# New planned durations and a newly searched order for a linear-attention and token-mixing kernel

## The chip, the cores and the metric

The kernel runs on one core of one Trainium2 chip. The metric is the device time of one execution in microseconds; the kernel before has a median of 141.56 us over 3 runs. PE is the matmul engine (TensorE), DVE is VectorE, ACT is ScalarE, POOL is GpSimd, and SP is SyncE, which here only issues DMAs.

## The reference

Two stages follow each other. The first is a linear attention with a decaying state, over 4 batches, 8 heads, 768 positions and a head size of 48:

```python
for t in range(S):
    kt, vt, rt = (k[:, :, t], v[:, :, t], r[:, :, t])
    cur = np.einsum('bhd,bhe->bhde', u[None] * kt, vt)
    y[:, :, t] = np.einsum('bhd,bhde->bhe', rt, state + cur)
    state = w[None, :, :, None] * state + np.einsum('bhd,bhe->bhde', kt, vt)
```

The second takes its output as x (4 batches, 768 tokens, 384 channels) and mixes tokens with two 768x768 matrices and channels with two 384x384 ones:

```python
theta = x @ w_theta
zr, zi = x * np.cos(theta), x * np.sin(theta)
y = np.einsum('ts,bsd->btd', w_tok_r, zr) + np.einsum('ts,bsd->btd', w_tok_i, zi)
u = x + y
out = u + np.maximum(u @ w_ch, 0.0)
```

## The kernel before

The 768 positions of a batch are cut into 6 chunks of 128 rows, taken two at a time. There are 12 such pairs, counted 0 to 11, three to a batch. A pair's work is called its front. Its k, r and v are loaded from SP into a ring of 9 tiles `ld` (L492, L499). k and r are multiplied by powers of w into Kw and Rw (L663), transposed on PE against an identity matrix ("flip", L553), and evacuated from PSUM to KT and RT (L562 on DVE, L564 on ACT). KT times RT gives the scores (L702), which DVE multiplies with a mask into mAT (L708). PD is RT times KT elementwise (L715), and one small matmul group ("diag", L724) sums it to dg; dg times v is yd (L732). Kw times v, the outer products, gives the state's sums (L747, or L761 for pairs 0 to 3); the state goes to N (L801) and, in bf16, to Sb. For pairs 0 to 3 the rows of v arrive two to a partition; they are cast to v2 (L616, L618) and placed by "put" matmuls (L627). Sb and mAT give the outputs (L821, L830), which with yd become x (L838).

x is transposed to xT, either by a flip or, for pairs 6 to 10, by a DMA transpose from SP (L573). theta is three matmuls a chunk against Wth (L853), followed by cosine and sine on ACT (L858, L861), and DVE multiplies x with both into z (L864).

The mixing of a batch needs the z of all its pairs. For each of 6 output chunks it runs 3 groups of 4 matmuls ("mix", L884), one group for each pair's z. DVE adds x (u, L891, kept in the tile uu_all), u is transposed by DMA for pairs 0 to 10, three matmuls against Wch follow (L907, "chan"), DVE finishes (fin, L911, the tile fin_all) and SP stores (L917).

The four weight matrices are loaded and cast to bf16 by DMAs that POOL issues (L512): Wth and Wch in one piece each, each token matrix (Wr for w_tok_r, Wi for w_tok_i) in three pieces of two row blocks. A piece lands in a tile that is idle then (z, x, uu_all, fin_all), and PE flips each of its two blocks into WrT or WiT. All casts stand behind a small copy on POOL, the gate (L687), that waits until the load of pair 2's r has landed.

The order of all this is not that of the code. Every piece of work is a task of a plan (`P.add`), with an engine, a planned duration, what it reads and writes, and how many of the 8 PSUM banks it takes. `Plan.order()` runs a small event-driven plan of the five engines and the two DMA queues (SP's and POOL's): whenever an engine is free it takes, among the tasks whose inputs are ready, the one with the lowest number. The numbers come from the list `RANK`, one for each of the 698 tasks, and `MOVED` names the tasks that go to their alternative engine (DVE instead of POOL, ACT instead of DVE, and so on). The order in which the tasks come out is the order in which the instructions are put on each engine. So the planned durations have no effect on the chip other than through this order: each engine runs its own instructions strictly in it, and each instruction waits for its inputs as they really arrive. The assignment of PSUM banks follows from the same run.

In the plan of before a DMA's result is ready 2000 ns (`LANDING`) after its data have gone through the planned queue. When both queues have transfers, each goes on at the share that the transfer of POOL's queue gives: 0.2 for SP and 0.9 for POOL with Wth and Wch, 0.13 and 0.95 with the token matrices. Tasks that use the SBUF port that DVE and POOL share (`port=True`) exclude each other in the plan; on the chip such a POOL instruction also waits for the last such DVE instruction that precedes it in the order.

Of the kernel before, what the change touches and what calls it, by code (L numbers as in the profile page):

```python
# [23 lines left out]
LAT = {PE: 230.0, DVE: 150.0, ACT: 250.0, POOL: 170.0, SP: 0.0}  # L24
SWITCH = 95.0
LANDING = 2000.0


class Task:
# [5 lines left out]
class Plan:  # L35
# [50 lines left out]
    def order(self):  # L86
# [23 lines left out]
        while times or dma_next < math.inf:  # L110
# [7 lines left out]
            while dma_at < now:  # L118
                live = [q for q in (0, 1) if queues[q]]
                if not live:  # L120
                    dma_at = now
                    break
                rate = self.rates(queues)
                q = min(live, key=lambda q: todo[q] / rate[q])
                need = todo[q] / rate[q]
                step = need if dma_at + need <= now + 1e-6 else now - dma_at
                for i in live:
                    todo[i] -= step * rate[i]
                if dma_at + need <= now + 1e-6:
                    dma_at += need  # L130
                    t = queues[q].pop(0)
                    todo[q] = queues[q][0].xfer if queues[q] else 0.0
                    t.end = dma_at + LANDING
                    release(t.users, t.end)
                else:
                    dma_at = now
            for e in engines:
                if free_at[e] > now:
                    continue
                shut = e in port_free and port_free[POOL if e == DVE else DVE] > now  # L140
                nfree = sum(1 for b in banks if b[0] <= now)
                t = min((t for t in waiting[e] if t.ready <= now and not (t.port and shut)
                         and not (t.acq and len(t.acq) + t.spare > nfree)),
                        key=lambda t: (t.prio, t.seq), default=None)
                if t is None:
                    continue
                waiting[e].remove(t)
                banks.sort()
                for b in t.acq:
                    self.bank_of[b] = banks.pop(0)[1]  # L150
                ns = t.ns
                if e == PE:
                    ns += SWITCH if t.mode != last_mode else 0.0
                    last_mode = t.mode
                t.start, done = now, now + ns
                free_at[e] = done
                if t.port:
                    port_free[e] = done
                heapq.heappush(times, done)
                out.append(t)  # L160
                if t.xfer > 0:
                    q = int(e == POOL)
                    queues[q].append(t)
                    if len(queues[q]) == 1:
                        todo[q] = t.xfer + ns
                else:
                    t.end = done + LAT[e] - min(t.xfer, 0.0)
                    for b in t.uses:
                        left[b] -= 1
                        freed[b] = max(freed.get(b, 0.0), t.end)  # L170
                        if left[b] == 0:
                            banks.append((freed[b], self.bank_of[b]))
                            heapq.heappush(times, freed[b])
                    release(t.users, t.end)
                release(t.nexts, done)
# [12 lines left out]
CAST_AFTER = 7  # L188

RANK = [  # L190
# [38 lines left out]
]  # L229

MOVED = [
    30, 32, 74, 77, 92, 97, 99, 182, 213, 222, 242, 257, 275, 280, 287, 364, 365, 368, 377, 382,
    396, 399, 428, 440, 516, 520, 529, 548, 551, 560, 580, 592, 595, 689,
]


# [15 lines left out]
def kernel(  # L252
# [260 lines left out]
              wr=keys, prio=prio, xfer=xfer, share=share, name="cast")  # L513

    def square(src, dst, key, prio, after):
        cast(dst, src.rearrange("(o p) n -> p o n", p=C), [key], prio, 1870, (0.2, 0.9), after)

    z1 = zs[1].rearrange("p o t n -> p (o t n)")
    landing = [(z1[:, 4 * S:], [("z", 1, 2)]),
# [9 lines left out]
    def token_weights(after):  # L529
        for q in range(NP):  # L530
            for key, src, dst in (("Wr", moe_w_tok_r, WrT), ("Wi", moe_w_tok_i, WiT)):
# [5 lines left out]
                for to in (2 * q, 2 * q + 1):  # L537
                    if (key, to) in W_BY_DMA:
                        P.add(SP, 1250, lambda dst=dst, mid=mid, to=to:
                              nc.sync.dma_start_transpose(out=dst[:, :, to * C:(to + 1) * C],  # L540
                                                          in_=mid[:, to % 2, :]),
                              rd=keys, wr=[(key, to)], prio=60 + to, xfer=900, name="turn")
                        continue
                    flip(dst[:, :, to * C:(to + 1) * C],
                         [mid[:, to % 2, s * C:(s + 1) * C] for s in range(NCH)],
# [25 lines left out]
    def turn(dst, src, tok, prio, rd, wr, by_dma):  # L571
        if by_dma:
            P.add(SP, 1250, lambda: nc.sync.dma_start_transpose(  # L573
                out=dst, in_=src.rearrange("p t n -> p (t n)")), rd=rd, wr=wr, prio=prio,
                xfer=900, name="turn")
        else:
            flip(dst, [src[:, t, dk * C:(dk + 1) * C] for t in range(2) for dk in range(ND)],
                 tok, prio, rd, wr)
# [3 lines left out]
    def front(b, base):  # L582
# [59 lines left out]
        for pr in range(NP):  # L642
# [71 lines left out]
            def pairwise(eng, PD=PD, RT=RT, KT=KT):  # L714
                eng.tensor_mul(PD, RT, KT)  # L715
            P.add(DVE, dve_ns(2 * HP * C, 2.0), lambda f=pairwise: f(nc.vector), rd=kKT + kRT,
                  wr=[kP], prio=pb + 4, port=True, name="PD",
                  alt=(POOL, 190 + 1.65 * 2 * HP * C, True, lambda f=pairwise: f(nc.gpsimd)))
            td = ("dg", g)

            def diag(td=td, PD=PD):
# [256 lines left out]
```

## Time and profile before

| what | us |
|---|---|
| median of 3 runs | 141.56 |
| lowest and highest of them | 141.51, 141.77 |
| the profiled execution, on the device | 142.75 |
| its span, from the first to the last instruction | 141.0 |
| busy in that span: PE, DVE, ACT, POOL | 125.4, 107.3, 76.6, 63.7 |

The profile is of one execution, and its times count from the first instruction. A row of a timeline or of the chain of waits begins with its start and its length in us. A group's row gives, behind a first bar, its busy time in us and the mean of one instruction in ns, then the idle time before it. Matmuls are pipelined, so their rows overlap: the chain of waits shows them without the overlap. "To landing" is the time from the issue of a DMA to the moment its semaphore tells of the data.

### The profile page before, as it was taken

The numbers are of one execution on the slowest core, as the hardware profiler recorded it, in microseconds if no ns is written. First come the engines' busy times: TensorE is split into PE (matmuls) and PEld (weight loads), VectorE is DVE, ScalarE is ACT, GpSimd is POOL, SyncE is SP. The second block draws the span as 40 slices with busy tenths as digits, with TensorE's granted clock in tenths as the row PEclk, the third lists the DMA queues.
The fourth block names the chain that finished last, engine by engine and source line by source line (L and its number), as shares of the span: only waits on it lengthen the run. The fifth ranks groups of instructions, "written<-read, shape, count | busy, mean of one in ns | idle before, by whom it ended". The sixth has DMA issues, their size and how long they took to land.

```text
span 141.0 us, 4099 instructions
## 1 busy us (share of the span) xinstructions
PE 125.4 (89%) x1677; PEld 84.1 (60%) x1677; DVE 107.3 (76%) x203; ACT 76.6 (54%) x142; POOL 63.7 (45%) x55
## 2 busy tenths in 40 slices
PE   1599989587999999999999999949899999999980
PEld 1377856374677577765677566726566556665640
DVE  5396999696474699999999999857986196446490
ACT  7967989958947860799434628535263400340010
POOL 6025599968050298594683879972500000000000
PEclk9999999999999999999999999999999999999998
DMA  2899999999995999999997999979984305412644
GB/s 68 234 325 327 247 240 170 214 199 190 197 211 133 195 200 167 191 176 196 156 233 127 207 254 173 245 118 241 198 210 150 69 8 161 105 67 48 175 167 167
DMA packets 72637, 25.24 MB, mean 179 GB/s; under 512 B 67241, under 2 KB 72618, under 8 KB 72618
## 3 DMA queue, kind: packets, MB, share of 16 engines
q1 hardware_dynamic: 70186, 22.03, 78.0%
q0 software_dynamic: 2432, 2.95, 11.9%
q8 instruction: 13, 0.21, 0.7%
q14 instruction: 6, 0.05, 0.2%
HBM read 20.06 MB, written 4.72 MB: 176 GB/s over the span
## 4 chain that ended last, share of the span: by engine, by line
PE 51%; DMA 19%; DVE 15%; POOL 7%; issue 4%; ACT 2%; DVEq 0%; POOLq 0%
PE bank L884 24%; DMA x<-in_moe_w_tok_i_dram 9%; PE bank L553 6%; PE bank L853 6%; DVE mAT L708 6%; PE bank L907 6%; DMA uu_all<-uu_all 5%; DMA xT<-x 4%; POOL yd L732 2%; DVE Rw L663 2%; DVE fin_all L911 2%; PE bank L702 2%; POOL PD L715 1%; PE bank L830 1%; DVE x L838 1%
## 5 line engine op out<-in xcount | busy, mean ns | idle before, releaser
L884 PE MATMUL bank<-z,WrT 128*128 128x384 bf16 x144 | 46.9, 326 | 0.0
L884 PE MATMUL bank<-z,WiT 128*128 128x384 bf16 x144 | 46.8, 326 | 0.0
L708 DVE TENSOR_TENSOR mAT<-bank,mask 128x512 bf16<-128x512 f32 x48 | 31.1, 681 | 2.4 <-PE bank L702 2.4
L884 PEld LDWEIGHTS <-WrT 128*128 128x128 bf16 x144 | 14.0, 97 | 8.0
L864 DVE TENSOR_TENSOR z<-x,trig 128x1536 bf16<-128x1536 bf16 x12 | 12.4, 1036 | 8.3 <-ACT trig L858 4.9
L884 PEld LDWEIGHTS <-WiT 128*128 128x128 bf16 x144 | 14.1, 98 | 7.7
L861 ACT ACTIVATE trig<-bank 128x384 f16<-128x384 f32 x24 | 11.6, 492 | 11.3 <-PE bank L853 5.6
L564 ACT ACTIVATE KT<-bank 128x1024 bf16<-128x1024 bf16 (+1 forms) x12 | 11.9, 989 | 10.2 <-PE bank L553 6.5
L715 POOL TENSOR_TENSOR PD<-RT,KT 128x1024 bf16<-128x1024 bf16 x7 | 14.9, 2127 | 5.5 <-ACT RT L564 3.2
L732 POOL TENSOR_TENSOR yd<-dg,vb 128x768 bf16<-128x768 f32 x10 | 14.7, 1475 | 6.0 <-DVE Rw L663 2.5
L891 DVE TENSOR_TENSOR uu_all<-bank,x 128x384 bf16<-128x384 f32 x24 | 13.2, 552 | 4.7 <-PE bank L884 4.4
L663 POOL TENSOR_TENSOR Kw<-ld,kpow 128x768 bf16<-128x768 f32 x7 | 12.7, 1815 | 8.8 <-DVE z L864 7.2
L907 PE MATMUL bank<-Wch,uu_all 128*128 128x384 bf16 x72 | 14.7, 326 | 2.0 <-DMA uu_all<-uu_all 1.9
L853 PE MATMUL bank<-Wth,xT 128*128 128x384 bf16 x72 | 14.4, 327 | 2.2 <-DMA Wth<-in_moe_w_theta_dram 1.8
L911 DVE SCALAR_TENSOR_TENSOR fin_all<-bank,uu_all 128x384 f32<-128x384 f32 x24 | 12.9, 552 | 4.1 <-PE bank L907 2.2
L663 POOL TENSOR_TENSOR Rw<-ld,rpow 128x768 bf16<-128x768 f32 x6 | 10.9, 1815 | 10.0 <-DVE z L864 5.2
L858 ACT ACTIVATE trig<-bank,pi 128x384 f16<-128x384 f32 x24 | 13.3, 582 | 3.5 <-PE bank L853 3.4
L838 DVE TENSOR_TENSOR x<-bank,yd 128x384 bf16<-128x384 f32 x24 | 12.3, 548 | 1.3 <-PE bank L830 1.3
L564 ACT ACTIVATE RT<-bank 128x1024 bf16<-128x1024 bf16 (+1 forms) x11 | 10.8, 985 | 1.8 <-PE bank L553 1.7
L907 PEld LDWEIGHTS <-uu_all 128*128 128x128 bf16 x72 | 6.6, 98 | 6.7 <-DMA uu_all<-uu_all 2.5
L853 PEld LDWEIGHTS <-xT 128*128 128x128 bf16 x72 | 6.3, 98 | 6.4 <-DMA Wth<-in_moe_w_theta_dram 1.9
L553 PE MATMUL bank<-ident,Kw 128*128 128x128 bf16 x96 | 8.4, 235 | 1.9 <-DVE Kw L663 1.7
(104 smaller groups left out, 185.7 us busy)
## 6 DMA issues: line engine op xcount, KB each, us to landing
ld<-in_r_dram SPq DMA_DIRECT2D x12, 384.0 KB, 6.1
out_dram<-fin_all SPq DMA_DIRECT2D x11, 384.0 KB, 2.7
ld<-in_k_dram SPq DMA_DIRECT2D x16, 192.0 KB, 4.8
ld<-in_v_dram SPq DMA_DIRECT2D x16, 192.0 KB, 5.9
ld<-in_k_dram SPq DMA_DIRECT2D x4, 384.0 KB, 4.9
ld<-in_v_dram SPq DMA_DIRECT2D x4, 384.0 KB, 4.7
fin_all<-in_moe_w_tok_i_dram POOLq DMA_DIRECT2D x1, 384.0 KB, 8.2
z<-in_moe_w_tok_r_dram POOLq DMA_DIRECT2D x1, 384.0 KB, 9.9
```

Of the source, the lines that this page charges most:

```text
L553: nc.tensor.matmul(bank16(tok)[:, i * C:(i + 1) * C], s, ident, is_transpose=True, start=(i == 0), stop=(i == n - 1))
L564: nc.scalar.activation(dst, src, Act.Copy)
L663: eng.tensor_mul(X[:, :, hs, :D], src[:, :, hs], pw[:, :, hs])
L708: P.add(DVE, dve_ns(HP * C), lambda hi=hi, tk=tk, mAT=mAT: nc.vector.tensor_mul(mAT[:, hi], bank(tk[hi]).rearrange("p (h t) -> p h t", h=H ...
L715: eng.tensor_mul(PD, RT, KT)
L732: eng.tensor_mul(yd.rearrange("p a h d -> p (a h) d"), wide(dg, D), vb.rearrange("p a h d -> p (a h) d"))
L838: P.add(DVE, dve_ns(HD), lambda hi=hi, ty=ty, yd=yd, pr=pr: nc.vector.tensor_add(x[:, 2 * pr:2 * pr + 2].rearrange("p a (h i e) -> p a h i ...
L853: nc.tensor.matmul(bank(th)[:, :HD], xT[:, t, dk, :], Wth[:, dk, :], start=(dk == 0), stop=(dk == ND - 1))
L858: P.add(ACT, act_ns(HD, False) + 65 + (1300 if g == 0 and t == 0 else 0), lambda th=th, t=t, trig=trig: nc.scalar.activation(trig[:, t, 0] ...
L884: nc.tensor.matmul(bank(tm)[:, :HD], (WrT, WiT)[ri][:, so, to * C:(to + 1) * C], z[:, so, ri], start=(part == 0 and i == 0), stop=(part == ...
L907: nc.tensor.matmul(bank(tf)[:, :HD], uT[:, t, dk, :], Wch[:, dk, :], start=(dk == 0), stop=(dk == ND - 1))
L911: nc.vector.scalar_tensor_tensor(fin[:, t], bank(tf)[:, :HD], 0.0, un[:, t], op0=Alu.max, op1=Alu.add),
```

## The change

These planned quantities are changed:

- a matmul task that starts before 11.2 us of the plan is held for 1.8 times as long;
- the cast of Wth is held for 3370 ns of transfer instead of 1870, and while it runs SP's queue goes on at 0.4 and POOL's at 0.95 (before 0.2 and 0.9); Wch stays as it was;
- a DMA transpose's transfer is held for 1000 ns instead of 900;
- and its result comes 1300 ns later than before;
- the product PD on POOL costs 190 + 1.9 ns an element column instead of 190 + 1.65.

RANK and MOVED are replaced by new lists. The number of tasks and what each computes stay as they are. 36 of the 698 tasks are now on another engine.

```diff
 LANDING = 2000.0
+SLOW_UNTIL = 11200.0
+TURN_LATE = 1300.0
...
-                    t.end = dma_at + LANDING
+                    t.end = dma_at + LANDING + (t.share[1] if q == 0 else 0.0)
...
                 if e == PE:
                     ns += SWITCH if t.mode != last_mode else 0.0
+                    ns *= 1.8 if now < SLOW_UNTIL else 1.0
...
 RANK = [
-    0, 361, 360, 363, 362, 364, 365, 366, 369, 372, 377, 367, 370, 368, 371, 382, 397, 383, 384,
+    0, 413, 412, 415, 414, 416, 417, 418, 421, 424, 429, 419, 422, 420, 423, 434, 408, 435, 436,
...
 MOVED = [
-    30, 32, 74, 77, 92, 97, 99, 182, 213, 222, 242, 257, 275, 280, 287, 364, 365, 368, 377, 382,
-    396, 399, 428, 440, 516, 520, 529, 548, 551, 560, 580, 592, 595, 689,
+    32, 40, 74, 84, 89, 94, 99, 112, 163, 172, 193, 197, 210, 213, 222, 234, 242, 245, 247, 275,
+    278, 365, 396, 408, 428, 440, 516, 548, 551, 580, 602, 691,
 ]
...
-        cast(dst, src.rearrange("(o p) n -> p o n", p=C), [key], prio, 1870, (0.2, 0.9), after)
+        cast(dst, src.rearrange("(o p) n -> p o n", p=C), [key], prio, 1870 + 1500 * (key == "Wth"), (0.4, 0.95) if key == "Wth"
+             else (0.2, 0.9), after)
...
-                xfer=900, name="turn")
+                xfer=1000, share=(1.0, TURN_LATE),
+                              name="turn")
...
-                  alt=(POOL, 190 + 1.65 * 2 * HP * C, True, lambda f=pairwise: f(nc.gpsimd)))
+                  alt=(POOL, 190 + 1.9 * 2 * HP * C, True, lambda f=pairwise: f(nc.gpsimd)))
```

In the new order, among what the prediction speaks of: POOL has Rw of pair 1, yd of pair 0, the gate, the casts of Wth, Wr 2-3 and Wch, then Kw of pair 3, the casts of Wi 0-1 and Wr 0-1, N, and the cast of Wi 4-5; two PD, a yd and a v2 cast follow, and then the casts of Wr 4-5 and Wi 2-3. Before, it had a v2 cast, Rw of pairs 1 and 2, yd of pair 0 and N ahead of the gate, and then the casts of Wth, Wi 2-3, Wr 0-1, Wi 0-1, Wch and Wi 4-5. On PE the first mixing group is the 56th group of tasks where it was the 57th. On SP the loads keep their order among themselves; around them, the small second load of w, with that of u, moves behind the first load of r, and late in the kernel the load of r of pair 8 moves behind the DMA transposes of u of pair 3 and x of pair 7, and the transpose of u of pair 5 moves ahead of a store.

More of the change, by code (lines that the diff above doesn't have):

```diff
@@ L541, in token_weights @@
                                                           in_=mid[:, to % 2, :]),
-                              rd=keys, wr=[(key, to)], prio=60 + to, xfer=900, name="turn")
+                              rd=keys, wr=[(key, to)], prio=60 + to, xfer=1000, share=(1.0, TURN_LATE),
+                              name="turn")
                         continue
@@ L574, in turn @@
                 out=dst, in_=src.rearrange("p t n -> p (t n)")), rd=rd, wr=wr, prio=prio,
-                xfer=900, name="turn")
+                xfer=1000, share=(1.0, TURN_LATE),
+                              name="turn")
         else:
```

74 rows, old and new, of the table RANK are left out of this document.

## The prediction

> **What bounds the kernel now.** I read the engine shares first, then a table of busy time by stage, then what TensorE (PE) waits for.
>
> ```profile
> PE 125.4 (89%) x1677; PEld 84.1 (60%) x1677; DVE 107.3 (76%) x203; ACT 76.6 (54%) x142; POOL 63.7 (45%) x55
> ```
>
> ```profile
> core 0: us, PE busy (x) PEld busy (x) DVE busy (x) ACT busy (x) POOL busy (x), PEclk, DMA share, GB/s
> 0.00:15.35 15.35, 10.61 (x142) 7.68 (x143) 10.13 (x34) 12.06 (x26) 4.96 (x13) 1.00 0.90 244
> 15.35:36.50 21.15, 17.15 (x331) 12.60 (x332) 17.81 (x33) 18.25 (x35) 18.02 (x17) 1.00 1.12 204
> 36.50:92.50 56.00, 55.65 (x864) 38.61 (x863) 50.34 (x86) 33.65 (x59) 35.00 (x22) 1.00 1.11 189
> 92.50:104.00 11.50, 9.12 (x107) 5.57 (x105) 8.83 (x17) 5.71 (x12) 5.72 (x4) 1.00 1.17 197
> 104.00:135.00 31.00, 30.97 (x231) 18.76 (x229) 17.85 (x31) 6.42 (x15) 0.00 (x0) 1.00 0.38 103
> 135.00:141.00 6.00, 1.94 (x13) 0.84 (x11) 2.34 (x5) 0.49 (x1) 0.00 (x0) 0.90 0.53 197
> ```
>
> PE does the same matmuls in either order, so the end can move only by PE's idle time: the stage's length less its busy time. That is 4.7 us before 15.35, 4.0 from there to 36.5 (where the first mixing matmul starts), 0.4 from 36.5 to 92.5, 2.4 from 92.5 to 104, nothing to 135, 4.1 at the end. The head and the tail are mostly latency, so 6.4 us can be argued over.
>
> ```profile
> PE bank L907 <- DMA uu_all<-uu_all: 1.9, 1, 1.9
> PE bank L853 <- DMA Wth<-in_moe_w_theta_dram: 1.8, 1, 1.8
> ...
> PE bank L553 <- DMA x<-in_moe_w_tok_i_dram: 1.0, 1, 1.0
> ...
> PE bank L853 <- DMA xT<-x: 0.5, 1, 0.5
> ```
>
> Each row gives who waited for what, the total, the times and the longest. PE waited for casts of the weights (Wth, the tok_i block that lands in x) and for DMA transposes (uu_all, xT). The edits change the planned durations of just these transfers, and of the early matmuls. The edits of durations issue nothing themselves; what changes on the chip is the order of the tasks, and the engine of 36.
>
> **The head, 0 to 15.35.** Up to the outer products of pair 1 both orders give PE the same groups, except that put(1,0) is in there before and diag(0) after. Prices of PE groups without overlap come from the chain of waits:
>
> ```profile
> 13.85 0.45 PE bank L553 x8
> 14.29 0.33 PE bank L627 x2
> 14.62 0.73 PE bank L761 x32
> 15.34 0.30 PE bank L724 x8
> ...
> 43.05 0.34 PE bank L553 x6
> 43.39 0.49 PE bank L853 x3
> ...
> 48.08 0.33 PE bank L702 x8
> ...
> 53.46 0.30 PE bank L821 x16
> 53.76 0.51 PE bank L830 x16
> ```
>
> Put (0.33) against diag (0.30) is nothing. ACT now evacuates the first KT half ahead of two tables and takes the cast of v2(0) from POOL, so RT and v2 come later; PE has the two puts and the first outer products in front of the scores meanwhile. I take +0.2, with ends of -0.3 (one diag or put hidden) and +0.7 (twice a put of 0.33, shown).
>
> The plan now holds early matmuls for 1.8 times slower until 11.2 us.
>
> ```profile
> 7.70 1.07 PE L553 MATMUL bank<-ident,Rw 128*128 128x128 bf16 x8
> ...
> 13.68 0.61 PE L553 MATMUL bank<-ident,Rw 128*128 128x128 bf16 x8
> ```
>
> The same eight flips take 1.07 us at 7.70 and 0.61 at 13.68, so the factor is right for this execution. The Trainium skill (TensorE: Matmul & The Clock Gate, Part 1) speaks against planning by it: the slow start is ended by a free-running activity window, it says, its place differs from run to run, and one should not fit to a cold count. By that rule the head's term would scatter around +0.2; no single trace can show it.
>
> **The casts, 15.35 to 36.5.** The start of the casts is set by POOL's queue.
>
> ```profile
> 15.63 1.82 POOL L663 TENSOR_TENSOR Rw<-ld,rpow 128x768 bf16<-128x768 f32 x1 [3.06 <-PE bank L724]
> 17.41 1.48 POOL L732 TENSOR_TENSOR yd<-dg,vb 128x768 bf16<-128x768 f32 x1
> ...
> 19.29 0.18 POOL L687 COPY gate<-ld 1x1 f32<-1x1 f32 x1
> 19.41 0.94 POOL L512 DMA_DIRECT2D Wth<-in_moe_w_theta_dram  x1
> ...
> 23.27 0.74 POOL L512 DMA_DIRECT2D z<-in_moe_w_tok_i_dram  x1
> ```
>
> After the change Rw of pair 2 is on DVE and N stands behind six casts; only yd(0) is left ahead of the gate. Its dg comes from diag(0), which PE now does before the second scores: behind diag stand scores 0.3, the state's column sums (16 matmuls, 0.5 or so by the 0.73 of 32), two flips 0.9 and outer products 0.7 before 15.5, so diag ends near 13.1, yd runs from 13.3 to 14.8 and Wth's cast is issued at about 15.1 instead of 19.4. N, 4.3 us of casts later, feeds only outputs(2), 36 PE groups further on. Kw of pair 3 (now on POOL) stands between the third and the fourth cast; it is the next to be late if its load is.
>
> ```profile
> z<-in_moe_w_tok_i_dram POOLq DMA_DIRECT2D x1, 384.0 KB, 15.3
> ...
> Wth<-in_moe_w_theta_dram POOLq DMA_DIRECT2D x1, 288.0 KB, 6.8
> ```
>
> Wth landed 6.8 after its issue (26.2), the sixth cast 15.3 after its own (38.6): five casts in 12.4 us, 2.5 apart. From 15.1 on that gives Wth at 21.9, then Wr 2-3 at 24.4, Wch (smaller) at 26.5, Wi 0-1 at 29.0, Wr 0-1 at 31.5, Wi 4-5 at 34.0.
>
> PE's arrival in the new order: from 15.5, put x4 (1.3), flips x4 (1.8), outputs without a state half (0.7), outer (0.7), a TX flip (0.3), scores x2 (0.7), diag (0.3): 5.8, so the first theta is reached at 21.3 and waits 0.6. To the Wr 2-3 flips come theta x2, scores x2 and outputs: 2.4, at 24.3, no wait. To Wi 0-1 another 3.5 (three flip groups, scores x2, diag, put, theta, outer): 27.9, waits 1.1. To Wr 0-1 another 1.5: 30.5, waits 1.0. Then three flip groups and two outputs (2.6) end at 34.1, when Wi 4-5 is there. Idle 2.7 in place of 4.0, and mixing starts near 34.5. I take **-1.3**. Ends: -3.4 if only the first wait stands (idle 0.6), +2.0 in the rival below.
>
> **The transposes, 92.5 to 104.**
>
> ```profile
> 85.59 0.75 SPq L492 DMA_DIRECT2D ld<-in_r_dram  x1
> 86.44 1.00 SPq L917 DMA_DIRECT2D out_dram<-fin_all  x1
> 87.53 1.75 SPq L573 DMA_TRANSPOSE uu_all<-uu_all  x1
> ```
>
> ```profile
> 87.53 7.17 DMA uu_all<-uu_all
> ...
> 96.53 4.97 DMA xT<-x
> ```
>
> The transpose of u of pair 3 took 7.17 us to land, xT of pair 8 4.97; PE stood 1.9 and 0.5 for them. On SP the new order puts the 384 KB load of r (85.59 here) behind both transposes instead of ahead, and the transpose of u of pair 5 ahead of an output. Were u's transpose as fast as xT's 4.97 it would land at 92.5, just as PE gets there: 1.9 gone. If the delay is the other traffic as such, nothing goes. Idle goes to something between 0 and 2.4; I take the middle, **-1.2**.
>
> **Middle and tail.** From 36.5 to 92.5 PE idles 0.4, so there is nothing to gain. DVE takes 18 tasks of other engines and gives 16, of the same kinds (Rw, PD, yd, evacuations): no term. At the end, two channel matmul groups now stand behind the last mixing group, and the last flip's evacuation goes from ACT to DVE.
>
> ```profile
> 137.08 0.56 DVE L911 SCALAR_TENSOR_TENSOR fin_all<-bank,uu_all 128x384 f32<-128x384 f32 x1 [0.20 <-PE bank L907]
> ```
>
> Before: the last fin ends 137.64, 3.0 after the last mixing (134.65), with 2.1 us of PE work behind it: 0.9 over. After: PE has 3.3 behind it and DVE un, six fins and one flip's evacuation (0.35 or so), of 0.55 each, so 4.2: 0.9 to 1.0 over, with one more 192 KB output at the end. The 0.5 that PE waited for ACT is gone, DVE's backlog takes its place: +0.1, from 0 to +0.4.
>
> **Sum.** +0.2 - 1.3 - 1.2 + 0.1 = -2.2 on a span of 141.0. The profiled execution took 142.75 on the device, 1.75 around its span and 1.2 above the median of the plain runs; what lies around the span is the same in both kernels, so the difference goes on the median: 141.56 - 2.2 = **139.4**.
>
> **Rivals.**
>
> *The earlier casts starve the loads (slower).* The casts will start while r of pair 3 is still coming.
>
> ```profile
> ld<-in_r_dram SPq DMA_DIRECT2D x12, 384.0 KB, 6.1
> ```
>
> ```profile
> L663 DVE TENSOR_TENSOR Rw<-ld,rpow 128x768 bf16<-128x768 f32 x5 | 5.5, 1110 | 0.0
> ```
>
> ```profile
> L492 SPq DMA_DIRECT2D ld<-in_r_dram x1: 1262/1262/1262, 19.1 to 19.1; - x1
> ...
> DMA to landing us min/median/max: 12.0/12.0/12.0
> ```
>
> The last load, issued with the first cast, took 12.0 us. If r of pair 3, issued at about 12.9, takes as long, it lands at 24.9, Rw on DVE adds 1.1, and PE, which reaches its flip at 20.6, stands 5.5; with 0.5 for later weights idle is 6.0, +2.0 over before. Sum: +0.2 + 2.0 - 1.2 + 0.1, that is 142.7. It decides against the change from a landing of 23.9 on (wait 4.4, idle 4.9). For it: DMA share is 1.12 in that stage. Against: the median load of r took 6.1 us, and most of r of pair 3 is through by 17, when Wth's data begin. The Trainium skill (DMA: Bandwidth & Descriptors, Queues, rings and completion order) says the DMA engines take turns between the queues by packets, which would slow the load without stopping it; the 12.0 above agrees.
>
> *DVE keeps the pace (same).* In the chain of waits DVE work leads nearly unbroken from 67 to 87.5, into the 7.17 us transpose. If DVE isn't earlier there, PE only waits the same time later: gains of both stages return as idle near 92. Time 141.56 + 0.3 - 0.3 = 141.6. For it: DVE 50.34 of 56. Against: DVE was idle 5.7 us there and 3.3 before, some of it for the casts.
>
> *Both stretches close.* Idle 1.2 in the cast stage (-2.8) and none for transposes (-1.9), +0.3 elsewhere: 137.2. For it: every wait named is one that the durations now cover. Against: two casts are still reached within 1 us of their landing.
>
> **How the numbers follow.** Forecast 0.50, loads starved 0.22, DVE keeps the pace 0.15, both close 0.13. About 0.2% (0.3 us) is what a measurement of this kernel can tell. Faster: 0.48 + 0.13 + 0.05; same: 0.02 + 0.05; slower: 0.22 + 0.05. The range 137.0 to 142.4 takes in the third and the fourth case and nearly half of the second; the forecast's own range is 138.2 to 140.8.
>
> **What would show it.** Wth's cast issued at 15 to 16 and landing by 22.5; first theta near 22; first mixing matmul at 33.5 to 35.5; PE idle of 2 to 3 us between 15 and there; u of pair 3 landing within 5.5 us. The forecast is wrong if the flip of r of pair 3 (L553) waits over 4 us, if the gate waits for its load beyond 17, or if PE shows new waits for DVE between 45 and 90, where it has none now.

## The result, and the profile after

| | before | after |
|---|---|---|
| median of 4 runs, us | 141.67 | 139.83 |
| lowest and highest | 141.51, 142.50 | 139.59, 140.21 |
| the profiled execution, on the device | 142.75 | 139.59 |
| its span | 141.0 | 137.9 |

The ratio is 0.986 with a 95% interval of 0.982 to 0.991: the changed kernel is faster by 1.8 us, where the prediction had 2.2. Here and below a median takes in all runs, and a ratio is of the means without the runs in a slower state that some executions of a kernel show. The two profiles differ by more (3.1), as that of before was taken in an execution 1.1 above its median. So a second pair of profiles was taken (runs e0 and e10 below, spans 140.5 and 138.5); where the two pairs differ, the text says so.

The page's first line and the stages of after, as in the prediction (start and end, length, then busy time of PE, PE's weight loads, DVE, ACT and POOL; the fifth row now ends with the last matmul):

```profile
PE 126.3 (92%) x1677; PEld 85.7 (62%) x1677; DVE 108.6 (79%) x205; ACT 75.5 (55%) x140; POOL 63.0 (46%) x55
```

```profile
0.00:15.35 15.35, 10.49 (x113) 7.51 (x113) 11.17 (x36) 11.22 (x24) 6.08 (x14) 1.00 0.91 246
15.35:36.50 21.15, 19.80 (x387) 14.89 (x387) 18.18 (x34) 17.76 (x33) 17.99 (x17) 1.00 1.18 221
36.50:92.50 56.00, 55.50 (x844) 38.55 (x842) 50.54 (x89) 34.90 (x60) 35.60 (x23) 1.00 1.21 191
92.50:104.00 11.50, 10.93 (x152) 6.94 (x151) 11.50 (x20) 5.70 (x13) 3.29 (x2) 1.00 1.03 171
104.00:133.57 29.57, 29.57 (x190) 17.86 (x188) 16.62 (x31) 5.95 (x13) 0.00 (x0) 1.00 0.39 110
133.57:137.90 4.33, 0.00 (x0) 0.00 (x0) 0.59 (x2) 0.00 (x0) 0.00 (x0) 1.00 0.57 208
```

PE's idle time by stage, length less busy, is the account of where the time came from. The last column is the same for the second pair.

| part | forecast | before, after | difference | second pair |
|---|---|---|---|---|
| PE idle, 0 to 15.35 | +0.2 | 4.74, 4.86 | +0.12 | +0.44 |
| PE idle, 15.35 to 36.5 | -1.3 | 4.00, 1.35 | -2.65 | -2.10 |
| PE idle, 36.5 to 92.5 | 0 | 0.35, 0.50 | +0.15 | +0.09 |
| PE idle, 92.5 to 104 | -1.2 | 2.38, 0.57 | -1.81 | -1.64 |
| 104 to the last matmul | 0 | 0.13, 0.00 | -0.13 | -0.10 |
| behind the last matmul | +0.1 | 3.96, 4.33 | +0.37 | +0.35 |
| PE busy in all | 0 | 125.44, 126.29 | +0.85 | +0.95 |
| sum | -2.2 | | -3.10 | -2.01 |

Two rows carry the gain, the stages of the casts and of the transposes. One row that the prediction had at nothing gives part of it back: PE is busy longer with the same matmuls.

PE's waits in after (who waited for what, total, times, longest):

```profile
PE bank L418 <- ACT z L409: 2.8, 1, 2.8
PE bank L558 <- DVE Kw L669: 1.4, 1, 1.4
PE bank L558 <- ACT trig L867: 1.1, 1, 1.1
PE bank L558 <- DVE Rw L669: 0.7, 1, 0.7
```

No row names a DMA any more: the waits for Wth, for the tok_i block and for the transposes are gone. The largest, for ACT, belongs to the first microseconds and was there before too. The wait of 1.1 us for ACT's trig work is new; it lies in the stage of the casts and is most of the 1.35 us of idle left there.

POOL's timeline shows the earlier casts as the prediction had them (start, length):

```profile
13.37 1.47 POOL L738 TENSOR_TENSOR yd<-dg,vb 128x768 bf16<-128x768 f32 x1
14.79 0.91 POOL L693 COPY gate<-ld 1x1 f32<-1x1 f32 x1
15.64 0.94 POOL L515 DMA_DIRECT2D Wth<-in_moe_w_theta_dram  x1
...
19.85 0.76 POOL L515 DMA_DIRECT2D x<-in_moe_w_tok_i_dram  x1
```

The page's DMA part gives its landing (last column, us from issue):

```profile
Wth<-in_moe_w_theta_dram POOLq DMA_DIRECT2D x1, 288.0 KB, 5.6
```

Wth's cast is issued at 15.64 instead of 19.41 and lands at 21.2 instead of 26.2. Then PE, in its timeline:

```profile
14.38 1.06 PE L558 MATMUL bank<-ident,Rw 128*128 128x128 bf16 x8
...
18.76 0.88 PE L558 MATMUL bank<-ident,Kw 128*128 128x128 bf16 x8
...
20.12 0.61 PE L558 MATMUL bank<-ident,Rw 128*128 128x128 bf16 x8
...
23.45 0.66 PE L859 MATMUL bank<-Wth,xT 128*128 128x384 bf16 x3
...
35.42 0.33 PE L890 MATMUL bank<-z,WrT 128*128 128x384 bf16 x1
```

The last two rows are the first theta, which no longer waits, and the first mixing matmul, at 35.42 (before: 36.49). The first three are eight flips of the same shape at three times. Before, they took 0.61 from 13.68 on; now they take 1.06 still at 14.38, 0.88 at 18.76, and 0.61 only at 20.12. The slow phase of PE's clock lasts about 6 us longer in the new order. The PEclk column of the stages shows 1.00 for all of this and doesn't tell of it; the flips do, and so does the trace's own record of the granted clock, which comes to full at 13.5 in before and 19.3 in after.

The late transposes on SP, and how long that of u of pair 3 took:

```profile
83.47 0.88 SPq L923 DMA_DIRECT2D out_dram<-fin_all  x1
84.45 1.26 SPq L578 DMA_TRANSPOSE uu_all<-uu_all  x1
85.81 1.25 SPq L578 DMA_TRANSPOSE xT<-x  x1
87.11 0.57 SPq L495 DMA_DIRECT2D ld<-in_r_dram  x1
```

```profile
DMA to landing us min/median/max: 5.7/5.7/5.7
```

It is issued 3.1 us earlier than before (87.53), and takes 5.7 instead of 7.17. In the second pair it is issued 2.0 us earlier (87.04, 85.03).

### The profile page after: what moved, and what is told of

It is laid out like the page before. It is cut to its first block, busy times and chain, and to the rows that moved or that the text cites. A ratio compares the mean times of both kernels' runs of the same rounds, so it can differ in the third digit from the quotient of the medians.

```text
span 137.9 us, 4097 instructions
## 1 busy us (share of the span) xinstructions
PE 126.3 (92%) x1677; PEld 85.7 (62%) x1677; DVE 108.6 (79%) x205; ACT 75.5 (55%) x140; POOL 63.0 (46%) x55
## 5 line engine op out<-in xcount | busy, mean ns | idle before, releaser
L714 DVE TENSOR_TENSOR mAT<-bank,mask 128x512 bf16<-128x512 f32 x48 | 30.5, 679 | 0.7 <-PE bank L708 0.3
L738 POOL TENSOR_TENSOR yd<-dg,vb 128x768 bf16<-128x768 f32 x12 | 17.7, 1475 | 10.4 <-ACT dg L735 7.8
L669 POOL TENSOR_TENSOR Kw<-ld,kpow 128x768 bf16<-128x768 f32 x8 | 14.6, 1820 | 14.8 <-DMA ld<-in_k_dram 8.4
L864 ACT ACTIVATE trig<-bank,pi 128x384 f16<-128x384 f32 x24 | 13.8, 584 | 10.7 <-PE bank L859 10.7
L870 DVE TENSOR_TENSOR z<-x,trig 128x1536 bf16<-128x1536 bf16 x12 | 13.7, 1143 | 1.5 <-ACT trig L864 1.2
L558 PE MATMUL bank<-ident,Rw 128*128 128x128 bf16 x96 | 8.4, 235 | 1.3 <-DVE Rw L669 0.7
```

The source lines that it names most:

```text
L558: nc.tensor.matmul(bank16(tok)[:, i * C:(i + 1) * C], s, ident, is_transpose=True, start=(i == 0), stop=(i == n - 1))
L669: eng.tensor_mul(X[:, :, hs, :D], src[:, :, hs], pw[:, :, hs])
L714: P.add(DVE, dve_ns(HP * C), lambda hi=hi, tk=tk, mAT=mAT: nc.vector.tensor_mul(mAT[:, hi], bank(tk[hi]).rearrange("p (h t) -> p h t", h=H ...
L738: eng.tensor_mul(yd.rearrange("p a h d -> p (a h) d"), wide(dg, D), vb.rearrange("p a h d -> p (a h) d"))
L864: P.add(ACT, act_ns(HD, False) + 65 + (1300 if g == 0 and t == 0 else 0), lambda th=th, t=t, trig=trig: nc.scalar.activation(trig[:, t, 0] ...
L870: P.add(DVE, dve_ns(4 * HD, 2.0) + 80, lambda trig=trig, pr=pr: nc.vector.tensor_mul(z[:, 2 * pr:2 * pr + 2], bc(x[:, 2 * pr:2 * pr + 2], ...
```

## The experiments

Each ratio is against the kernel before, timed on the same chip: medians 141.56 for e3 to e6, 141.05 for e1, e2, e7 and e8, 141.75 for e0 and e9 to e11. Several kernels take the finished order of one kernel and move a few tasks in it, so that all the rest stays frozen:

```diff
     order = P.order()
+    def shift(seqs, behind):
+        for seq in seqs:
+            t = P.tasks[seq]
+            order.remove(t)
+            order.insert(order.index(P.tasks[behind]) + 1, t)
+            behind = seq
```

**The theory** going in: the gain of the first stage comes from the earlier gate alone, and that of 92.5 to 104 from the load of r that moved behind the transposes. Rivals: loads starved by earlier casts eat the gain; the gain needs the whole new order; the transposes were late for no reason of their own.

### e0: before again

The kernel before, for a second profile.

> The kernel before, unchanged, for a second profile: the first one took 1.2 us more than the median. Theory (the waits for DMA transposes near 92.5 to 101.5 belong to this order): 1.5 to 2.5 us of PE idle between 92.5 and 104 again. Rival (they belonged to that execution): under 0.7 us there. Full clock at 13 to 16.5 us.

One execution took 142.21, span 140.5. PE's waits:

```profile
PE bank L853 <- DMA Wth<-in_moe_w_theta_dram: 1.9, 1, 1.9
PE bank L907 <- DMA uu_all<-uu_all: 1.8, 1, 1.8
```

They stand within 0.1 of the first profile (1.8, 1.9), so they belong to the order and not to one execution. The flips tell something else:

```profile
13.69 1.06 PE L553 MATMUL bank<-ident,Rw 128*128 128x128 bf16 x8
...
16.58 0.61 PE L553 MATMUL bank<-ident,Kw 128*128 128x128 bf16 x8
```

At 13.7 they are still slow, where the first profile had 0.61 at 13.68. The end of the slow phase moves between executions of one kernel.

### e3: after, with the gate late

Kw of pair 3 goes ahead of the gate on POOL; nothing else moves.

```diff
+    shift([210], 110)
```

> The changed kernel with one task moved: Kw of pair 3 goes ahead of the gate on POOL, so the casts start after it, near 19.5 us instead of 15.6, as late as before the change; everything else keeps its place. Theory (the early start of the casts is worth the idle time between 15 and 36 us): that idle time rises from 1.35 us to 3.5 to 5 and the time from 139.8 to 141.8 to 143. Rival (the gain comes from the new order of PE and DVE, the casts had slack): idle under 2 us, time within 0.5 of 139.8.

Median 141.87 of 12 runs, ratio 1.003 (1.0005 to 1.006). POOL, PE's waits, and the stage:

```profile
19.62 0.94 POOL L515 DMA_DIRECT2D Wth<-in_moe_w_theta_dram  x1
```

```profile
PE bank L558 <- DMA uu_all<-in_moe_w_tok_r_dram: 1.1, 1, 1.1
PE bank L859 <- DMA Wth<-in_moe_w_theta_dram: 0.8, 1, 0.8
PE bank L558 <- DMA z<-in_moe_w_tok_r_dram: 0.7, 1, 0.7
```

```profile
15.35:36.50 21.15, 18.09 (x312) 12.70 (x310) 16.30 (x30) 16.88 (x31) 16.33 (x17) 1.00 1.14 210
```

One instruction of 1.8 us, which itself waits 2.75 for its load, ahead of the gate takes away the whole gain. The waits for weights are back, and PE's idle in the stage is 3.06 instead of 1.35, a little less than the 3.5 to 5 expected. The first mixing matmul comes at 38.57, later even than before (36.49). In the new order the early casts are necessary. The stage of the transposes has no waits here either, though the casts are late; its row stands at the end of the next section.

### e4 and e9: before, with the gate early

e4 is the opposite edit: in the order of before, the gate, Wth's cast and the one behind it go directly behind Rw of pair 1, ahead of Rw of pair 2, yd of pair 0 and N. e9 adds three moves that put the work on v of pair 3 (its cast, puts and outer products, and the next two loads into its ring tile) later.

```diff
+    shift([68, 69, 85], 130)
```

```diff
+    shift([68, 69, 85], 130)
+    shift([226, 194, 227, 228, 195, 229], 121)
+    shift([196, 197], 217)
+    shift([193, 350, 351], 215)
```

> The kernel before with the gate and the first two casts (Wth, Wi 2-3) moved on POOL to behind Rw of pair 1, into a stretch where POOL idles from 12.6 to 15.6; nothing else is moved. Theory: Wth's cast is issued near 14.5 instead of 19.4, the waits of PE for Wth (1.8) and for later casts (1.4) go, and the time falls from 141.6 by 1.5 to 2.5. Rival (the order of PE and DVE makes the gain): under 0.5 less. Second rival (earlier casts starve the loads of pair 3): 0.5 to 2 slower.

> The kernel before with the early casts of the experiment above, and with the work on v of pair 3 moved later: its cast on ACT (and the two loads that reuse its tile on SP) behind the evacuation of RT of pair 3, its outer products, puts and their evacuations behind the first two theta groups. Theory (early casts pay only where PE's order leaves the late load of v of pair 3 its time): the wait of 2.1 us for that cast goes, and the time falls to 0.7 to 2 us under before. Rival (the remaining reordering makes the gain): within 0.5 of before.

e4: median 142.26, ratio 1.003 (0.999 to 1.007). e9: median 142.29, ratio 1.004 (0.9995 to 1.008). No gain in either; the theory had 1.5 to 2.5 us for e4 and 0.7 to 2 for e9, and fell both times. (The profile of e4 is of its fastest run, 140.99.) In e4 Wth landed at 20.1 and PE no longer waited for it, but v of pair 3, issued 0.75 us behind Wth's cast, took 8.3 us to land (5.2 in before). PE's waits and its timeline in e4 (the bracket is the idle time ahead and its releaser):

```profile
PE bank L761 <- ACT v L616: 2.1, 1, 2.1
```

```profile
24.36 0.80 PE L761 MATMUL bank<-v,Kw 64*64 64x48 bf16 x32 [2.14 <-ACT v L616]
...
26.32 1.06 PE L553 MATMUL bank<-ident,Rw 128*128 128x128 bf16 x8
```

The wait has an aftermath. In the stretches around it the clock (the third number from the end) falls:

```profile
22.00:25.00 3.00, 0.86 (x36) 0.75 (x33) 2.21 (x4) 1.54 (x3) 0.77 (x2) 1.00 1.21 251
25.00:30.00 5.00, 5.00 (x60) 2.92 (x56) 3.01 (x6) 4.86 (x11) 3.92 (x3) 0.66 1.20 193
```

PE was busy for only 0.86 of 3 us, and soon after, the clock record stands at half from 26.25 to 29.66; the flips at 26.32 take 1.06 again. On top of the wait of 2.1, PE worked at half speed for 3.4 us; that is 1.7 us of work lost, by an estimate from these two numbers, about what the early casts were to bring. It is not this execution alone: the mean granted clock is 0.988 or less in all 12 runs of e4 and all 12 of e9, in 10 of the 40 runs of before beside them, and in none of the 16 of the changed kernel and e5. That the wait brings the fall is argued from the order in time. It is no simple rule: PE was busy for only 1.25 us between 23.5 and 26.5 in the profile of before, and its clock did not fall.

e9 has no wait for v, but others that weren't there:

```profile
PE bank L724 <- DVE PD L715: 0.8, 2, 0.6
PE bank L553 <- POOL Rw L663: 0.8, 1, 0.8
```

```profile
15.35:36.50 21.15, 17.04 (x339) 12.38 (x334) 16.94 (x32) 16.37 (x30) 15.75 (x16) 0.92 1.16 218
25.00:28.50 3.50, 3.50 (x26) 1.80 (x28) 2.65 (x5) 2.54 (x3) 3.44 (x3) 0.51 1.18 203
```

Idle in the stage is 4.11, and the clock falls again. So early casts are not sufficient: in the old order they hold up a load that PE needs, and with the work on that load moved, other waits open.

One thing that differs in the new order is the place of the casts among the loads. In e4 and e9 Wth's cast (14.45 and 15.35) is issued ahead of the last load of pair 3, v (15.16 and 15.58), which lands 8.3 and 9.6 us later. In after v is issued at 14.06, 1.6 us ahead of Wth's cast (15.64), and lands in 5.9, as r of pair 3 does that is issued at 12.9 (second pair: v at 13.74, cast at 15.81, 6.1 us). The old order with its casts right behind the load of v was not run. So it is not shown whether the early casts need the new order of PE, DVE and ACT beside them, or only the loads of pair 3 ahead of them.

The next r load in after, issued at 18.7 beside the casts, took 17.0 (landings of the line of the loads from 18 to 19):

```profile
DMA to landing us min/median/max: 17.0/17.0/17.0
```

It is r of pair 4, landing at 35.7, and no row of PE's waits names it. In the second pair it took 16.3; in e3, where it is issued at 18.87, ahead of the casts, 4.9. The loads are slowed beside the casts, more than in the prediction's rival (12.0), but the order has nothing that needs them by then.

The late stage of e3, e4 and e9, in this order:

```profile
92.50:104.00 11.50, 11.46 (x168) 7.69 (x163) 11.50 (x21) 6.04 (x13) 5.21 (x4) 1.00 0.58 128
```

```profile
92.50:104.00 11.50, 11.42 (x127) 7.19 (x124) 11.04 (x20) 6.66 (x14) 5.83 (x4) 1.00 1.11 208
```

```profile
92.50:104.00 11.50, 11.26 (x156) 7.40 (x154) 10.98 (x20) 6.54 (x14) 7.06 (x5) 1.00 1.04 183
```

PE idles 0.04, 0.08 and 0.24 us there, where before had 2.38. All three reach the first mixing matmul later than before (38.57, 37.20 and 38.69 against 36.49). So the two stages are not independent: a PE that has lost time ahead of the mixing finds the transposes landed (in e9 that of u of pair 3 is even issued 0.55 us later than before, at 88.08, and PE doesn't wait for it), and the idle time of the one stage can't be added to that of the other as if each stood alone.

### e5: after, with the load of r ahead of the transposes

The prediction's reason for the late stage, undone.

```diff
+    shift([513], 512)
```

> The changed kernel with the load of r of pair 8 put back on SP to its old place, ahead of the store and the DMA transposes of u of pair 3 and x of pair 7. Theory (that load delays the transposes): u of pair 3 lands 1 us or more later than now (90.1) and the time rises by 0.3 to 1.5. Rival (the transposes have slack now, or are slowed by all traffic alike): within 0.3 of 139.8.

Median 139.74 of 6 runs, ratio 0.987 (0.983 to 0.991): the same as after. u of pair 3 is issued at 85.97, 1.5 us later than in after, and takes 6.75 instead of 5.7: it lands at 92.7 instead of 90.1. One short wait appears:

```profile
PE bank L913 <- DMA uu_all<-uu_all: 0.4, 1, 0.4
```

So the load of r does delay the transpose, by 2.6 us, as the prediction had it, but the new order has room for all but 0.4 of that, and the median shows nothing. e4 and e9 have the load of r in its old place (82.93 and 84.57, ahead of u of pair 3 at 86.46 and 88.08) and no wait for this transpose. The gain of the stage doesn't need the move of that load. Nor does the earlier transpose need the early casts: in e3, with late casts, u of pair 3 is issued at 82.45, 2.0 us earlier than in after.

### e1 and e2: durations and lists taken apart

e1 has the new durations with the old RANK and MOVED, e2 the old durations with the new lists.

> The changed planned durations with the old RANK and MOVED. The order comes out of both, so it is a third order. Theory (the gain needs an order of PE that fits the early casts, which the search found): no gain, 141 to 143. Rival (the durations alone correct the order): 139.5 to 140.5.

> The old planned durations with the new RANK and MOVED. POOL's queue starts its casts as early as in the changed kernel, and PE's order differs in places. Theory (the lists carry the early casts and most of the fitting order): 139.5 to 141. Rival (lists and durations only work together): 141.5 or more.

e1: median 150.81, ratio 1.067 (1.062 to 1.072). e2: median 156.19, ratio 1.099 (1.090 to 1.108). e1 came out far above both of its theories; e2 agrees with its rival, which set no upper end. The largest wait behind the head's in e1, then in e2:

```profile
PE bank L558 <- DMA fin_all<-in_moe_w_tok_i_dram: 2.0, 1, 2.0
```

```profile
PE bank L884 <- DVE z L864: 3.1, 2, 2.5
```

No single wait explains losses of this size. In both profiles PE is also busy some 5 us longer (131.48 and 131.27 up to 150 us, against 126.29 in after): the clock record stands at half from 33.0 to 39.8 and from 63.7 to 67.1 in e1, and from 29.1 to 32.5 and from 138.3 to 141.7 in e2. The mean granted clock is 0.986 or less in all runs of both.

A list of priorities means an order only together with the durations under which it was searched. Taken apart, either half gives a third order that nobody searched, so the gain can't be split between the two.

### e6, e7, e11, e10: a longer start for PE

Matmuls on a constant tile, whose results nothing reads, are put into PE's idle places in the head: in after (e6, and the same kernel again as e11) 7 of them, in before (e7) 6. e10 is the changed kernel again, beside e11.

```diff
+    def busy(n):
+        for _ in range(n):
+            nc.tensor.matmul(bank_t[7], junk[:, :C], junk, start=True, stop=True)
+    busy(3)
...
+        busy({14: 3, 55: 1}.get(t.seq, 0))
```

> The changed kernel with 7 extra matmuls of 128x512 on a constant tile in PE's idle time of the head (3 ahead of the first matmul, 3 behind the second group, 1 behind the flip of the second half of k), whose result nothing reads. Theory (the clock record starts at full clock at 19.3 us in the changed kernel and at 13.5 before, and the slow matmuls up to there cost some 2 us): with PE busy earlier the full clock comes before 13 us and the time falls by 1 to 2.5 us, to 137.5 to 138.8. Rival (PE waits for its inputs in the head whatever the clock, or the instant does not depend on PE's activity): within 0.3 of 139.8.

> The kernel before with 6 extra matmuls of 128x512 on a constant tile in the idle time of PE's head (3 ahead of the first matmul, 1 behind the second group, 1 behind the transpose of w and u, 1 behind the first flip), whose result nothing reads. Theory (the new order gains by its casts, and gives part of it away by a later full clock): the old order has its full clock at 13.5 to 16 already and waits for the casts behind it, so it gains less than the changed kernel's 0.8, 0 to 0.5 us. Rival (a slow head costs both orders the same): 0.6 to 1.2 us faster than before.

> The changed kernel, unchanged, beside the others on the same chip: 1 to 2% under before; full clock at 18 to 22 us.

> The changed kernel with the 7 extra matmuls in the head, once more, beside the changed kernel itself. Theory (an earlier full clock is worth part of a microsecond): 0.4 to 1.2 us under the changed kernel, full clock before 13 us. Rival: within 0.3 of it.

| run | median, us | ratio | full clock in its profile from |
|---|---|---|---|
| e6 | 138.94 | 0.983 (0.978 to 0.987) | 8.0 |
| e5, beside e6 | 139.74 | 0.987 (0.983 to 0.991) | 21.6 |
| e11 | 139.38 | 0.984 (0.978 to 0.990) | 21.1 |
| e10, beside e11 | 139.92 | 0.988 (0.982 to 0.994) | 21.35 |
| e7 | 141.03 | 1.000 (0.997 to 1.004) | 15.3 |

The flips of e6 are fast at 12.59 already, those of e10 as late as in after:

```profile
12.59 0.62 PE L558 MATMUL bank<-ident,Kw 128*128 128x128 bf16 x8
```

```profile
18.92 1.06 PE L558 MATMUL bank<-ident,Kw 128*128 128x128 bf16 x8
...
21.05 0.76 PE L558 MATMUL bank<-ident,Rw 128*128 128x128 bf16 x8
...
22.88 0.62 PE L558 MATMUL bank<-ident,Kw 128*128 128x128 bf16 x8
```

Both times the kernel with the extra matmuls is faster than its neighbour, by 0.8 and 0.5, and its two ratios are the lowest of all; e6 gained less than the 1 to 2.5 us that its theory had. But the intervals overlap, and in e11's profile the clock came as late as without them: how much of the gain is the clock's stays open. In before they did nothing, and there the clock was not earlier either.

### e8: after, with the column sums later

One suspect for the longer slow phase: the state's column sums, 16 small matmuls that stand at 12.82 in after, in the middle of the head (8.71 in before). They go behind the first outer products of pair 1.

```diff
+    shift([63, 64], 143)
```

> The changed kernel with the 16 one-column matmuls of the state's column sums (0.8 us in which PE streams next to nothing) moved on PE, with their evacuation on ACT, behind the outer products of pair 1. Theory A (these in the middle of the head keep PE's activity low and the full clock late): full clock between 11 and 17 us instead of 19.3 to 21.6, time 0.4 to 1.2 us under 139.8. Rival (something else of the head decides): full clock at 19 to 22 again, time within 0.4 of 139.8.

Median 139.32, ratio 0.989 (0.985 to 0.993), as after's 0.986. The flips:

```profile
18.76 1.06 PE L558 MATMUL bank<-ident,Kw 128*128 128x128 bf16 x8
...
20.37 0.61 PE L558 MATMUL bank<-ident,Rw 128*128 128x128 bf16 x8
```

Full clock comes at 19.8, within the range of the changed kernel (19.3 to 21.35). Going by this one profile, it isn't the column sums.

## Why the prediction was right, step by step

**The casts** (-1.3). The mechanism was right: N and Rw of pair 2 are gone from POOL's queue ahead of the gate (N stands behind five casts, where the prediction counted six), Wth is issued 3.8 us earlier (15.64, forecast 15.1), lands at 21.2 (21.9) and PE stops waiting. e3 shows that this step is necessary, e4 and e9 that it is not sufficient, which the prediction didn't say. The size was off: idle fell by 2.1 to 2.65, not 1.3. The reason is a second error that is linked with it: PE was to reach the first theta at 21.3 and wait; on the slow clock it came at 23.45, when the weights were there. The first mixing matmul comes 1.07 earlier in the first pair (36.49 to 35.42) and at the same time in the second (36.14, 36.15), where the forecast had 2.0 (34.5). The new order has some 19 and 17 more matmuls done by then, which leaves PE 0.6 and 0.7 us less to do; even so 1.7 and 0.7 us are gained up to there, less than the idle time alone says. The slow clock turns part of the saved waiting into longer work.

**The head** (+0.2). No group was hidden and no wait was added: +0.12 and +0.44 of idle, inside the ends. What failed is the premise "PE does the same matmuls in either order, so the end can move only by PE's idle time": PE's busy time rose by 0.85 and 0.95, and the flips show the slow clock to last longer in the head. The Trainium skill (TensorE: Matmul & The Clock Gate, Part 1) advises not to fit to a cold count, and the prediction made of it a scatter around +0.2. The runs agree with the advice and show more than scatter: full clock came at 13.5 to 16.0 in five profiles with the order of before or small edits of it (the two of before, e4, e7, e9), at 19.3 to 21.9 in six with that of after (after, e3, e5, e8, e10, e11). The 11.2 us of the plan hold in neither order.

**The transposes** (-1.2). The gain is there in both pairs (-1.81, -1.64), within the range that was given (0 to 2.4 of idle left), but the step "the new order puts the 384 KB load of r behind both transposes" is not what it rests on (e5, e4, e9). u of pair 3 is issued 3.1 us earlier (2.0 in the second pair); by e3 this comes from the new order without the early casts, and which part of that order does it stays open. The two stages are also linked, which the sum of the prediction left out: kernels that reach the mixing later (e3, e4, e9) have no wait here. In this stage DVE is now busy for 11.50 of 11.50 us, where it had 8.83: it may be what is late next.

**The tail** (+0.1). +0.37 and +0.35, at the upper end, but not by DVE's backlog. PE's and DVE's last rows in after:

```profile
131.45 2.11 PE L913 MATMUL bank<-Wch,uu_all 128*128 128x384 bf16 x12
...
132.14 2.02 DVE L917 SCALAR_TENSOR_TENSOR fin_all<-bank,uu_all 128x384 f32<-128x384 f32 x4
```

The last fin ends at 134.16, 0.6 us behind the last matmul; before, it ended at 137.64, also 0.6 behind (137.04). The added time stands behind the last fin, where only stores are left: 3.40 us to the end before, 3.73 after (3.41 and 3.72 in the second pair). What makes it longer is not shown.

**The rivals.** *Starved loads*: r of pair 3 landed at 18.8, far from the 23.9 at which the rival decides, so it was wrong for this change; for the edit alone, in the old order, v of pair 3 was held up in the place of r (e4), with a time that is not clear of noise from before's. The Trainium skill (DMA: Bandwidth & Descriptors, Queues, rings and completion order) says that the DMA engines take turns between queues by packets; 17.0 us for r of pair 4 beside the casts, against 5.9 for r of pair 3, agrees with a load that is slowed and not stopped. *DVE keeps the pace*: PE's idle from 92.5 to 104, where the saved time was to come back as waiting, fell by 1.81 and 1.64, so no. *Both stretches close*: nearest in the stages themselves (idle 1.35 and 0.57), but the slow clock and the tail took back 1.2, which it had at 0.3.

**The sum.** -2.2 was forecast; -3.10 and -2.01 in the two pairs of profiles and -1.84 in the medians. The forecast came out near because two terms that were too small (casts, transposes) stood against two that were missing or small (busy time, tail). That they balanced is luck.

**What stays open**: what in the new head keeps the clock slow for 6 us longer; what in the new order issues u of pair 3 earlier; whether casts right behind the last load of pair 3 would pay in the old order; and why e11 had no early clock with the same instructions as e6.

## What to carry to other kernels

When durations are re-measured, search the order again with them: durations and priorities are one thing, and mixing two sets cost 6.7 and 9.9% here. Before counting a wait as gained by an earlier transfer, look for the loads that it will share the DMA engines with, and for whether they are issued ahead of it or behind. Don't add up waits of stages that follow each other as if each stood alone. Make the account with PE's idle time by stage and its busy time beside it, and don't plan by a clock phase read from one trace of another order.

## What the runs showed of the hardware

- The slow start of PE's clock lasted until 13.5 to 16.0 us in one order and 19.3 to 21.9 in another of the same matmuls; two profiles of one kernel lay 1.75 (before, e0) and 2.04 apart (after, e10). Eight flips took 1.06 in it and 0.61 behind it.
- The clock also fell back in the middle of a kernel: after 0.86 us of PE work in 3 us (e4) it stood at half for 3.4 us, and in e9 at 0.51 from 25.0 to 28.5. In before 1.25 us of work in 3 us brought no fall.
- The same instructions (e6 and e11) had full clock from 8.0 us in one profile and from 21.1 in another.
- Beside the weight casts a 384 KB load took 17.0 and 16.3 us (after, e10); the same load issued just ahead of them took 4.9 (e3).
